# First norm's sums of ten tiles moved to ScalarE, the column tiling of chunk 1's projections dropped, another issue order

## The chip, the cores and the metric

One core of a Trainium2 chip. The metric is the device time of one execution in microseconds (us); a kernel is given by the median of its executions. PE is the matmul engine, DVE VectorE, ACT ScalarE, POOL GpSimd, SP the engine that issues transfers. All executions compared here were of the fast state (mean granted clock of PE, as a share of full speed, 0.98 to 1.00).

## The reference, cut to what matters

```python
mod = (_silu(c) @ w_mod).reshape(c.shape[0], 6, 1, -1)      # sa, ca, ga, sb, cb, gb
h = _layernorm(x, axis=-1) * (1 + ca) + sa                  # first norm, x is 2048 x 512
x = x + ga * _A_ref(h, A_wqkv, A_wo)                        # 32 heads, window of 8 keys, step 2
h = _layernorm(x, axis=-1) * (1 + cb) + sb                  # second norm
x = x + gb * _B_ref(h, B_w1, B_b1, B_w2, B_b2)              # a third norm, then an MLP over the rows
```

x is held as 16 tiles of 128 rows. Attention goes through five chunks of 2, 4, 4, 4 and 2 tiles. Its products (q by k, weights by v) are elementwise on DVE, which PE then sums up.

## The kernel before: the parts that matter

The kernel records every operation with a name and issues the operations in the order of one long string. A suffix picks an engine (`:a` ACT, `:d` DVE, `:p` POOL) or, for matmuls, `:q`: four column tiles side by side. Each engine takes its operations strictly in this order. In names, `ln1s4` is the statistics of tile 4 for the first norm, `n1_4` its normalisation, `qk1_0` a q-k product of chunk 1, `pv4_3` a product with v of chunk 4, `ev` an eviction from PSUM, `wsc` the scaling of a weight block, `x_1_4` a load of two tiles of x from tile 4.

```python
ORDER = """
ld_x_1_2 ident ld_c act_table ld_x_1_4 ld_x0 consts warm2 ld_x_2_8 ld_x1 cps ld_x_2_6 silu_exp ld_wmod1 ln1s3
...  (cut)
"""
    NE=('PAPADADAAADAAAPA', 'AAPPAPAAAAAAPAAA', 'APPAAADDDDDDDADD'),  # engine of each tile's normalisation, three norms
    VPOOL=(2, 3),                                                       # two blocks of the v weights scaled on POOL
...  (cut)
    def ln_stats(l, st, src, reads, name):
        st6, mv = ln_t["st6", l], ln_t["mv", l]

        def fd():
            nc.vector.bn_stats(st6[:, st, :], src)
            nc.vector.bn_aggr(mv[:, st, :], st6[:, st, :])
        return add("dve", 0.86, fd, reads=reads, writes=[("mv", l, st)], name=name)
...  (cut: ln_norm)
        alts = {"A": ("act", 0.8, lambda: nc.scalar.activation(dst, src, ACT.Identity, scale=r_, bias=n_)),
                "D": ("dve", 0.42, lambda: nc.vector.tensor_scalar(dst, src, args[0], args[1], op0=args[2], op1=args[3])),
                "P": ("pool", 0.8, lambda: nc.gpsimd.tensor_scalar(dst, src, args[0], args[1], op0=args[2], op1=args[3]))}
        G.add_any([alts[e]], reads=reads, writes=writes, name=name, locks=True)
```

Of the kernel before, what the change touches and what calls it, by code (L numbers as in the profile page):

```python
# [7 lines left out]
ACT = mybir.ActivationFunctionType  # L8
# [33 lines left out]
class _Graph:  # L42
# [7 lines left out]
    def add(self, eng, dur, fn, **kw):  # L50
        return self.add_any([(eng, dur, fn)], **kw)
# [131 lines left out]
ld_x_1_2 ident ld_c act_table ld_x_1_4 ld_x0 consts warm2 ld_x_2_8 ld_x1 cps ld_x_2_6 silu_exp ld_wmod1 ln1s3  # L183
ld_wqkv1 ln1s5 ld_wqkv0 ld_x_3_10 ln1s4 ln1s2 ln1s0 rstd1_1 ln1s1 ld_wmod0 ln1s9 rstd1_0 nb1_0 nb1_1 silu_dve
n1_1 n1_0 ld_x_4_14 ln1s6 n1_5 n1_2 fill:2:114 tr0_0 ln1s8 modcols1 n1_3 halo0 ld_wqkv2 n1_4 hT0_3:a hT0_1:d
hT0_0:a ld_x_3_12 fill:4:11 tr1_2 a1col hT0_2:d wsc1_0:a wsc1_1:d tr1_0 ld_wo3 wsc1_3:d wsc1_2:d hT1_3:a ln1s7
qkv0_12 hT1_1:a ld_wmod5 wsc0_0:a wsc0_1:d qkv0_10 wsc0_3:d ld_b2 rstd1_2 wsc0_2:d ln1s10 ld_wmod4 hT1_0:a
qkv0_00 ev0_10:a ln1s11 ev0_12:a modcols0 ld_wo0 nb1_2 qkv0_02 sab hT1_2:d ld_wmod3 n1_6 qvb0 ln1s15 qkv1_02
qvb_cp0 ln1s14 wsc2_2 ev0_02:a qvb1 ln1s13 wsc2_3 qkv1_10 wsc2_1:a wsc2_0:a qvb_cp1 qk0_3 qkv1_00 ev0_00:a
qkv0_22 qk0_2 ev1_02:a qkv1_01 ev1_10:a qk0_0 qkv0_20 ev1_01:a qk0_1 ev1_00:a red0_0 xt6 qkv1_12:q n1_9 qk1_0  # L190
ev0_20:a red0_1 red0_2 ld_wo1 red0_3 mask ev1_12:a ld_wmod2 qkv1_13:q n1_7 qkv1_03 max0 n1_8 xt7 qk1_2 qkv1_11
ev1_03:a xt9 sub0 qkv1_23 ev1_11:a exp0 qkv1_21 qk1_1 ev1_13:a xt8 ev0_22:a esum0 qkv1_22:q ld_b1 rcp0 halo_v1:p
rstd1_4 vd0_1 smB0 qkv1_20 qk1_3 a2_0_1 modcol2 a2_0_0 ev1_20:a red1_0 ev1_23:a a2_0_2 red1_1 ev1_22:a red1_2
a2_0_3 ln1s12 red1_3 ev1_21:a ld_wo2 qkv2_00 mcols0 nb1_4 max1 rstd1_3 n1_14 vd0_0 n1_15 qkv2_10 vd0_2 nb1_3
ev2_00:a n1_10 sub1 pv0_1 ev2_10:a xt10 qkv2_01 n1_12 qk2_0 mrowt0 qkv2_02 exp1 vd1_3 qkv2_11 vd0_3 ev2_01:a
n1_11 vd1_2 qkv2_22 pv0_2 ev2_11:a xt12 qkv2_12 mrows0:a ev2_02:a qk2_1 pvacc0_2 xt11 ev2_12:a red2_0 n1_13
esum1:q halo_v2:p xt13 qkv2_13:q rcp1 qk2_2 ev2_22:a qkv2_03:q vd1_1 ev2_13:a qkv2_23:q ev2_03:a smB1 qkv2_20:q
qk2_3 a2_1_3 red2_1 ev2_20:a a2_1_2 qkv3_01:q halo_k3:a ev2_23:a a2_1_0 red2_2 a2_1_1 qkv3_13 pv0_0 ld_w1_0_896
red2_3 st_row0 pv0_3 ev3_13:a qkv2_21:q vd1_0 max2 pvacc0_0 ev2_21:a qkv3_10:q pv1_3 pvacc0_1 sub2:q oev0_0:a
qkv3_23:q ev3_10:a exp2 qkv3_00:q ld_row0 pv1_2 xt14 ev3_01:a qkv3_02:q ev3_00:a qkv3_20:q vd2_0 ev3_23:a vd2_1  # L200
esum2:q pv1_0 ld_w1_0_0 qkv3_21 rcp2 pvacc0_3 qkv3_03:q woq_s oev0_2:a ev3_02:a pvacc1_3 ev3_03:a smB2 qkv3_11:q
pv1_1 a2_2_2 wo1:q ev3_11:a a2_2_1 ev3_21:a wo0 xt15 x1_1 halo_v3:a qk3_1 pvacc1_1 oev1_3:a a2_2_0 pvacc1_0 x1_0
a2_2_3 qkv3_12 oev1_1:a ld_w1_0_512 oev1_0:a qk3_0 pvacc1_2 vd2_2 modcol3 oev1_2:a vd2_3 ev3_12:a ln2q0 wo4
qk3_3 wo5 x1_4 ln2q1 qkv4_12 mcols1 ev3_20:a qk3_2 red3_0 ln2q4 red3_1 qkv3_22:q ln2m0 wo3 ev3_22:a pv2_1 x1_5
mrowt1 wo2:q mrows1:a x1_3 st_row1 red3_2 pv2_0 x1_2 pvacc2_1 rstd2_0 red3_3 ln2q2 qkv4_02:q oev2_1:a ld_row1
nb2_0 max3 n2_0 vd3_3 ev4_02:a vd3_0 pv2_3 sub3 vd3_2 qkv4_10 exp3 pvacc2_0 n2_1 esum3 pv2_2 ln2q3 qkv4_20
ev4_12:a qkv4_22:q rcp3 ev4_20:a ln2m2 pvacc2_2 aff0 warm3 oev2_0:a oev2_2:a qkv4_00:q smB3 rstd2_2 ln2q5 nb2_2
pvacc2_3 ln3s0 a2_3_1 n2_2 warm1 ev4_22:a a2_3_0 ln3s1 n2_3 biascols oev2_3:a a2_3_2 ln2m4 ev4_10:a aff2 wo7:q
a2_3_3 rstd2_4 ld_w2_1 rstd3_0 wo6:q nb2_4 nb3_0 ln3s2 n2_4 n2_5 h3_0 vd3_1 ln3s3 wo8:q h3_1 x1_6 aff4 warm0
rstd3_2 x1_7 wo9:q nb3_2 ln3s4 h3_2 h3_3 x1_8 ln3s5 halo_v4:p mlp1_0_2_0:q vd4_1 ev4_00:a pv3_0 mlp1_0_5_0:q  # L210
x1_9 mlp1_0_1_0:q rstd3_4 ln2q9 mlp1_0_0_0:q nb3_4 pv3_3 biascols_cp:a vd4_2 h3_5 pvacc3_0 h3_4 mlp1_0_6_0:q
ln2q8 mlp1_0_0_4:q pv3_2 mlp1_0_1_4:q vd4_3 park0_0:a mlp1_0_5_4:q mlp1_0_2_4:q park0_1:a mlp1_0_4_0:q ln2q7
park0_2:a pv3_1 mlp1_0_3_0:q vd4_0 ln2q6 mlp1_0_3_4:q oev3_0:a pvacc3_2 park0_3:a ld_w1_0_1152 pvacc3_3 oev3_2:a
ln2m6 mlp1_0_4_4:q qk4_0 oev3_3:a pvacc3_1 rstd2_6 mlp1_0_7_0:q oev3_1:a nb2_6 qk4_2 red4_0 n2_9 mlp1_0_6_4:q
wo13:q n2_7 qk4_1 ld_w1_0_1408 n2_6 wo12:q qk4_3 n2_8 park0_4:a red4_1 red4_2 aff6 red4_3 ld_w2_3 park0_5:a
wo11:q x1_12 mlp1_0_9_0:q ln2q12 park0_6:a wo10:q max4 x1_11 ld_w2_0 ln3s8 x1_13 sub4:q mlp1_0_10_0 ln3s7 exp4
x1_10 ln3s6 esum4 mlp1_0_11_0 ln3s9 rcp4 mlp1_0_12_0 smB4 rstd3_6 ln2m12 a2_4_3 ln2q10 h3_7 mlp1_0_8_0 h3_6
a2_4_1 rstd2_12 h3_8 mlp1_0_8_4 ln2q13 a2_4_2 nb2_12 h3_9 n2_12 ln2q11 a2_4_0 ln2m13 mlp1_0_9_4 ln2m10 rstd2_13
aff12 mlp1_0_7_4 rstd2_10 nb2_10 ln2m11 mlp1_0_7_8 ln3s12 rstd2_11 mlp1_0_8_8 n2_10 mlp1_0_9_8 pv4_0
ld_w1_0_1664 mlp1_0_11_4 park0_7:a rstd3_12 nb2_13 pv4_2 mlp1_0_10_4 park0_8:a n2_13 mlp1_0_10_8 nb2_11 pv4_1  # L220
mlp1_0_11_8 park0_9:a ld_w1_1_0 mlp1_0_12_4 park0_10:a pv4_3 mlp1_0_12_8 park0_11:a pvacc4_2 pvacc4_0 park0_12:a
aff10 pvacc4_1 pvacc4_3 n2_11 mlp1_0_13_0 aff13 ld_w2_5 oev4_0:a mlp1_0_13_4 aff11 oev4_2:a mlp1_0_13_8 inj1_0
wo15 ln3s10 wo14 ln3s13 rstd3_10 ln3s11 park0_13:a mlp1_1_0_6 x1_15 ld_w1_1_640 rstd3_13 ld_w1_1_896 rstd3_11
ln2s15 inj1_4 inj1_2 inj1_3 mlp1_1_3_6 nb3_13 h3_10 rstd2_15 nb2_15 mlp1_1_2_6 x1_14 n2_15 ln2s14 h3_13
mlp1_1_3_10 inj1_1 mlp1_1_0_10 mlp1_1_1_6 aff15 rstd2_14 nb2_14 mlp1_1_2_10 ln3s15 n2_14 mlp1_1_4_6 park1_0:a
h3_12 mlp1_1_1_10 aff14 inj1_5 rstd3_15 inj1_6 mlp1_1_4_10 mlp1_1_5_6 ln3s14 ld_w1_1_1408 mlp1_1_6_6 h3_11
rstd3_14 h3_15 park1_1:a h3_14 mlp1_1_6_10 mlp1_1_5_10 park1_2:a mlp1_1_10_10 ld_w1_2_0 park1_3:a mlp1_1_9_10
park1_4:a padd1_10 park1_5:a mlp1_1_7_10 park1_6:d ld_w2_7 mlp1_1_12_10 mlp1_1_8_10 padd1_12 padd1_9 mlp1_2_1_11
padd1_7 ld_w1_2_640 mlp1_2_1_14 gelu9 mlp1_2_2_11 gelu7 mlp1_2_4_11 ld_w2_4 gelu10 mlp1_2_4_14 mlp1_2_0_11
gelu12 padd2_4 mlp1_2_2_14 padd2_1 mlp1_2_0_14 padd2_2 mlp1_2_3_11 ld_w2_9 padd2_0 mlp1_2_3_14 gelu1 mlp1_2_6_11  # L230
padd1_8 gelu0 mlp1_2_5_11 padd2_6 gelu4 gelu2 mlp1_2_5_14 padd2_3 mlp1_1_13_10 padd2_5 gelu6 ld_w2_2 gelu8
mlp1_1_11_10 padd1_13 gelu5 gelu3 mlp2_0_0 padd1_11 gelu11 ld_w2_11 mlp2_0_0b gelu13 mlp2_0_0c mlp2_4_0 fin0_0
st_out0_0 mlp2_2_0 mlp2_8_0 fin2_0 fin4_0 st_out2_0 mlp2_1_0 st_out4_0 ld_w2_13 fin8_0 mlp2_7_0 fin1_0 st_out1_0
mlp2_5_0 st_out8_0 mlp2_11_0 mlp2_3_0 mlp2_6_0 fin3_0 fin5_0 st_out3_0 mlp2_9_0 st_out5_0 fin6_0 fin7_0
st_out6_0 ld_w2_15 mlp2_10_0 fin9_0 st_out9_0 st_out7_0 mlp2_14_0 fin10_0 st_out10_0 fin11_0 mlp2_12_0
st_out11_0 fin14_0 mlp2_13_0 st_out14_0 fin12_0 mlp2_15_0 fin13_0 mlp2_15_1 st_out13_0 fin15_0 st_out12_0
mlp2_15_2 fin15_1 st_out15_0 fin15_2 st_out15_1 st_out15_2
# [4 lines left out]
def kernel(  # L242
# [22 lines left out]
    NE=('PAPADADAAADAAAPA', 'AAPPAPAAAAAAPAAA', 'APPAAADDDDDDDADD'),  # L265
    X1D=(14, 15),
    LN2D=(14, 15),
# [100 lines left out]
    def ln_stats(l, st, src, reads, name):  # L368
        st6, mv = ln_t["st6", l], ln_t["mv", l]

        def fd():
            nc.vector.bn_stats(st6[:, st, :], src)
            nc.vector.bn_aggr(mv[:, st, :], st6[:, st, :])
        return add("dve", 0.86, fd, reads=reads, writes=[("mv", l, st)], name=name)
# [230 lines left out]
    def build_chunk(ch):  # L605
# [26 lines left out]
        if ch in XDMA:  # L632
            first = None
            for sl, st in enumerate(tiles):
                dma_t = lambda sl=sl, st=st: nc.sync.dma_start_transpose(out=hT[:, :, sl * P:(sl + 1) * P],
                                                                         in_=h3[:, st, :])
                add("sp", 1.25, dma_t, reads=[("n1", st)] + ([("hT_raw", bh)] if sl else []),
                    writes=[("hTr", ch, sl)] + ([] if sl else [("hT_raw", bh)]), bytes_=0.5, lat=1.2, desc=8,
                    name=f"xt{st}")
# [378 lines left out]
```

## Time and profile before

| | before |
|---|---|
| time, median of the first 3 executions | 207.41 us (207.18 to 207.63) |
| profiled span | 205.1 us |

The busy times and PE's standstill before stand in the prediction below. A busy time is the sum of an engine's instructions. Two groups by shape that the prediction doesn't show, of the kernel before (after the bars: busy us, mean ns, then the idle time ahead of them and what ended it):

```profile
L133 POOL TENSOR_SCALAR h<-xx,rs,nb 128x512 bf16<-128x512 bf16 x7 | 5.4, 780 | 73.2 <-DVE nb L133 73.2
L133 DVE TENSOR_TENSOR big<-q_sb,k_f 128x2048 bf16<-128x2048 bf16 x8 | 9.3, 1220 | 0.0
```

POOL does nine normalisations here, the seven of this group at 0.78 us each, and the q-k products of two tiles take DVE 1.22 us.

### The profile page before, as it was taken

The numbers are of one execution on the slowest core, as the hardware profiler recorded it, in microseconds if no ns is written. First come the engines' busy times: TensorE is split into PE (matmuls) and PEld (weight loads), VectorE is DVE, ScalarE is ACT, GpSimd is POOL, SyncE is SP. The second block draws the span as 40 slices with busy tenths as digits, with TensorE's granted clock in tenths as the row PEclk, the third lists the DMA queues.
The fourth block names the chain that finished last, engine by engine and source line by source line (L and its number), as shares of the span: only waits on it lengthen the run. The fifth ranks groups of instructions, "written<-read, shape, count | busy, mean of one in ns | idle before, by whom it ended". The sixth has DMA issues, their size and how long they took to land.

```text
span 205.1 us, 5082 instructions
## 1 busy us (share of the span) xinstructions
PE 196.7 (96%) x2089; PEld 106.7 (52%) x2089; DVE 162.6 (79%) x258; ACT 118.0 (58%) x271; POOL 15.4 (7%) x36
## 2 busy tenths in 40 slices
PE   7999999997999997999999999999999999999994
PEld 6988654453553644644555444444444444444453
DVE  2989999999999999999999899964563262066845
ACT  2396897983768788989999796673682000000000
POOL 4112007120000000230000100000000000000000
PEclk9999999999999999999999999999999999999999
DMA  5999684796859839073389149559992045006202
GB/s 170 303 375 298 156 174 113 219 261 183 247 180 283 243 141 357 27 190 147 121 220 219 27 97 336 187 125 291 274 300 67 29 135 146 0 26 165 81 26 78
DMA packets 55114, 35.98 MB, mean 175 GB/s; under 512 B 24628, under 2 KB 52404, under 8 KB 55092
## 3 DMA queue, kind: packets, MB, share of 16 engines
q1 hardware_dynamic: 55084, 35.67, 63.1%
q8 instruction: 16, 0.26, 0.5%
q14 instruction: 6, 0.05, 0.1%
q10 hardware_dynamic: 8, 0.00, 0.0%
HBM read 22.55 MB, written 2.10 MB: 120 GB/s over the span
## 4 chain that ended last, share of the span: by engine, by line
PE 52%; DVE 31%; issue 6%; ACT 5%; DMA 3%; SPq 2%; DVEq 0%
PE psS L133 50%; DVE big L133 17%; DVE h L133 5%; DVE st L133 4%; DVE mv L133 2%; PE psL L133 2%; ACT h L133 2%; SPq L133 2%; DMA xx<-in_A_x_dram 1%; DMA a2sb<-lsb 1%; ACT xx L133 1%; DVE lsb L133 1%; DVE m L133 1%; ACT q_sb L133 1%; DVE nb L133 0%
## 5 line engine op out<-in xcount | busy, mean ns | idle before, releaser
L133 PE MATMUL psS<-h,wst 128*32 128x512 bf16 (+1 forms) x374 | 51.1, 379 | 0.4 <-POOL h L133 0.2
L133 PE MATMUL psS<-hT,w_qkv 128*32 128x512 bf16 (+3 forms) x516 | 46.9, 346 | 1.5 <-ACT v_sb L133 1.1
L133 PEld LDWEIGHTS <-wst 128*128 128x128 bf16 (+1 forms) x476 | 29.6, 98 | 30.2 <-issue 2.2
L133 PEld LDWEIGHTS <-w_qkv 128*32 128x32 bf16 (+1 forms) x558 | 29.8, 109 | 22.3 <-issue 3.8
L133 DVE TENSOR_TENSOR big<-a2sb,vD 128x4096 bf16<-128x4096 bf16 (+1 forms) x20 | 36.5, 1861 | 0.2
L133 DVE TENSOR_TENSOR big<-q_sb,k_f 128x4096 bf16<-128x4096 bf16 (+1 forms) x20 | 36.4, 1861 | 0.0
L133 DVE SCALAR_TENSOR_TENSOR h<-psS,bcol,rows_bc 128x512 f32<-128x512 f32 (+2 forms) x18 | 12.4, 691 | 23.2 <-PE psS L133 22.9
L133 PE MATMUL psS<-gT,big 128*128 128x512 bf16 x112 | 24.8, 379 | 0.0
L133 PEld LDWEIGHTS <-ident 128*128 128x128 bf16 (+1 forms) x301 | 15.5, 104 | 6.7 <-issue 2.1
L133 PEld LDWEIGHTS <-big 128*128 128x128 bf16 x144 | 12.0, 98 | 13.2
L133 ACT ACTIVATE h<-xx,nb,rs 128x512 bf16<-128x512 bf16 x22 | 17.2, 808 | 1.7 <-DVE nb L133 1.7
L133 PE MATMUL psS<-woq,o_sb 128*32 128x512 bf16 (+1 forms) x184 | 16.5, 380 | 0.4 <-ACT xx L133 0.4
L133 DVE TENSOR_TENSOR psS<-psS,gT 128x512 f32<-128x512 f32 x14 | 9.0, 694 | 8.0 <-PE psS L133 8.0
L133 DVE BATCH_NORM_STATS2 st<-xx 128x6 f32<-128x512 bf16 x18 | 12.2, 677 | 3.8 <-DMA xx<-in_A_x_dram 3.7
L133 ACT ACTIVATE v_sb<-psS,qvb 128x512 bf16<-128x512 f32 (+1 forms) x20 | 11.2, 598 | 4.3 <-PE psS L133 4.2
L133 ACT ACTIVATE lv<-mv,epscol 128x1 f32<-128x1 f32 (+2 forms) x25 | 7.3, 292 | 11.0 <-DVE mv L133 10.8
L133 PE MATMUL psS<-ident 128*128 128x128 bf16 x161 | 12.0, 242 | 1.4 <-POOL epscol L133 1.4
L133 ACT ACTIVATE q_sb<-psS,qvb 128x512 bf16<-128x512 f32 (+1 forms) x20 | 11.1, 599 | 2.8 <-DVE qvb L133 1.9
L133 DVE TENSOR_TENSOR h<-h,xx 128x512 bf16<-128x512 f32 (+2 forms) x18 | 11.4, 632 | 1.6 <-DMA out_dram<-h 1.0
L133 ACT ACTIVATE gT<-psS,bcol 128x512 bf16<-128x512 f32 x14 | 8.7, 684 | 7.0 <-DVE psS L133 7.0
L133 DVE TENSOR_TENSOR h<-h,rows_bc 128x512 bf16<-128x512 bf16 (+2 forms) x20 | 11.5, 581 | 0.3
L133 PEld LDWEIGHTS <-group 128*32 128x32 bf16 x288 | 7.0, 96 | 8.8 <-issue 2.7
(89 smaller groups left out, 213.9 us busy)
## 6 DMA issues: line engine op xcount, KB each, us to landing
vD<-v_sb SPq DMA_DIRECT2D x12, 524.5 KB, 4.6
big<-in_B_w_dram SPq DMA_DIRECT2D x4, 896.0 KB, 8.1
vD<-v_sb SPq DMA_DIRECT2D x8, 268.5 KB, 2.6
wst<-in_B_w_dram SPq DMA_DIRECT2D x3, 640.0 KB, 4.4
out_dram<-h SPq DMA_DIRECT2D x15, 128.0 KB, 1.8
xx<-in_A_x_dram SPq DMA_DIRECT2D x7, 256.0 KB, 6.9
wst<-in_B_w_dram SPq DMA_DIRECT2D x2, 800.0 KB, 4.8
gT<-in_w_mod_dram SPq DMA_DIRECT2D x3, 512.0 KB, 8.3
```

Source lines behind the costliest of these rows:

```text
L133: r = fn(*a, **k)
```

## The change

Its intent: ACT stands idle for half of the first 20 us while DVE is full; so let ACT make the sums of ten tiles of x by two passes (the mean, the mean of squares), and let DVE only combine them. The order and the engine letters are new throughout; the three column-tiled projections of the first two chunks, all of chunk 1, run at full width.

```diff
-ld_x_1_2 ident ld_c act_table ld_x_1_4 ld_x0 consts warm2 ld_x_2_8 ld_x1 cps ld_x_2_6 silu_exp ld_wmod1 ln1s3
+ld_c ld_x_1_4 ident act_table ld_x_1_2 ld_x0 consts warm2 ld_x_2_6 ld_x_2_8 cps ld_x1 ld_wmod1 ln1s5 halo0
 ...  (cut: the rest of the order)
-    NE=('PAPADADAAADAAAPA', 'AAPPAPAAAAAAPAAA', 'APPAAADDDDDDDADD'),
+    NE=('DDPDPDAAAPADPAAA', 'PAPPAPAAAAAAAPPA', 'PAPAAADDAPDADPDP'),
+    LN1A=(4, 5, 6, 7, 8, 9, 10, 11, 12, 13),
 ...  (cut)
+        if l == 0 and st in LN1A:
+            def fa():
+                nc.scalar.activation(junk[:], src, ACT.Identity, scale=1.0 / D, accum_out=mv[:, st, 0:1])
+                nc.scalar.activation(junk[:], src, ACT.Square, scale=D ** -0.5, accum_out=st6[:, st, 0:1])
+            add("act", 1.36, fa, reads=reads + ["act_table"], writes=[("sq", l, st)], name=name)
+            add("dve", 0.15, lambda: nc.vector.scalar_tensor_tensor(
+                mv[:, st, 1:2], mv[:, st, 0:1], mv[:, st, 0:1], st6[:, st, 0:1], op0=ALU.mult, op1=ALU.subtract,
+                reverse1=True), reads=[("sq", l, st)], writes=[("mv", l, st)], name="ln1v" + name[4:])
+            return
 ...  (cut: options that stay unused, estimates of durations)
```

## The prediction

> **What bounds the kernel now.** I read four views of the profile before, in this order: the busy table, a table of engine times in stretches of 5 us, the chain of waits, and the groups by shape.
>
> ```profile
> PE 196.7 (96%) x2089; PEld 106.7 (52%) x2089; DVE 162.6 (79%) x258; ACT 118.0 (58%) x271; POOL 15.4 (7%) x36
> ```
> PE looks full and DVE four fifths full, but these are means over stages. The stretches (columns: stretch, its length, then PE, PEld, DVE, ACT, POOL busy, granted clock, DMA share, GB/s) tell the stages apart:
> ```profile
> 5.00:10.00 5.00, 5.00 (x85) 5.00 (x83) 4.72 (x18) 1.55 (x5) 0.47 (x1) 1.00 0.95 298
> ...
> 15.00:20.00 5.00, 5.00 (x77) 4.37 (x75) 4.86 (x16) 3.05 (x8) 1.16 (x2) 1.00 1.11 306
> ...
> 35.00:40.00 5.00, 5.00 (x30) 2.36 (x23) 4.93 (x9) 4.86 (x10) 0.76 (x1) 1.00 0.64 180
> ...
> 160.00:165.00 5.00, 5.00 (x25) 2.28 (x24) 2.13 (x3) 0.00 (x0) 0.00 (x0) 1.00 0.01 2
> ```
> DVE is full from 3.7 us to about 136 us and half idle after it. ACT is idle half the time in the first 20 us (1.55 and 3.05 of 5) but full at 35 to 40. That hole is what the change wants to fill. The chain of waits (start, length, what) agrees at both ends:
> ```profile
> 3.71 0.70 DVE st L133
> 4.41 0.02 issue
> 4.43 0.18 DVE mv L133
> 4.62 0.59 DVE st L133
> ...
> 123.50 75.54 PE psS L133 x355
> ```
> The first norm's sums stand on the chain at once when x lands (0.59 + 0.20 us a tile, seven tiles to 9.4 us). From 123.5 us the chain is 75.5 us of matmuls back to back, 355 of them at 0.213 us: nothing but less matmul work after that point, or an earlier start of it, shortens it. The start is when DVE has done the last product of chunk 4.
>
> How much can PE gain at all? Adding the starts of neighbouring matmuls in the timeline, PE stands still for only some 6.3 us in all; the two largest are these:
> ```profile
> 48.38 1.06 PE L133 MATMUL psS<-hT,w_qkv 128*32 128x512 bf16 x16 [1.06 <-ACT v_sb L133]
> ...
> 78.55 0.59 PE L133 MATMUL psL<-m,nident 128*128 128x512 bf16 x2 [1.49 <-DVE m L133]
> ```
> and it loses about 0.09 us at each of some 30 changes between full-width and column-tiled matmuls (2.7 us), and about 10 us to filler matmuls on the identity at the start. So no more than 6 to 8 us can be won by any reordering, and DVE and PE are close to co-bound before 123 us.
>
> **What the Trainium skill says.** "ScalarE: Activation LUTs", section What ACT_TABLE_LOAD costs, gives an ACTIVATE with immediate scale and bias as 186 ns + 0.833 ns per column, and 93 ns of overlap between neighbours: 613 ns at 512 columns. The trace agrees: the second norm's Square pass takes 622 ns and starts 0.62 us before the next instruction with its accumulator read counted.
> ```profile
> L133 ACT ACTIVATE junk<-xx 128x512 bf16<-128x512 bf16 x14 | 8.7, 622 | 0.1
> L133 ACT ACTIVATION_READ_ACCUMULATOR junk<-xx 128x1 f32 x14 | 2.7, 192 | 0.0
> L133 DVE BATCH_NORM_STATS2 st<-xx 128x6 f32<-128x512 bf16 x18 | 12.2, 677 | 3.8 <-DMA xx<-in_A_x_dram 3.7
> L133 DVE CAST gT<-psS 128x512 bf16<-128x512 f32 x1 | 0.7, 680 | 0.0
> ```
> "TensorEngine Tiling (Array Packing)", Key Properties, says that a change of tiling mode drains the array; the 0.09 us per change is what the trace shows of it. "Trainium Kernel Development and Optimization", Performance Expectations, calls matmul busy time a bad metric; here 96% does overstate, though by little. "DMA: Bandwidth & Descriptors", section Queues, rings and completion order, says that each of the 16 engines takes descriptors in ring order. The trace fits: in the order of issue the x tiles landed at 4.38 (512 KB in all by then), 6.57 (896 KB), 7.04 (1024 KB) and 8.60 us (1280 KB).
>
> **The change part by part.**
>
> *DVE.* Up to the last attention product (chunk 4) I count its instructions in the two orders and price them by the spacing in the trace. Ten pairs of BN statistics go: 10 x 0.80 = -8.0. Ten one-column variance instructions come (like the one-column ones at about 150 ns, spaced 0.13): +1.3. Four evictions of q and k from PSUM move from ACT to DVE: 4 x 0.68 = +2.7. Two more transposed chunk-1 copies (0.33), two more first-norm applications (0.38), one more weight scaling (0.26): +1.7. Two fewer third-norm applications: -0.6. Sum -2.9 us out of 117.9. So most of what ACT takes over is handed back.
>
> *ACT.* +10 x 1.23 = 12.3 us; minus 4 normalisations (2.8), 2 copies (0.95), 2 evictions (1.2), 1 scaling (0.6): +6.7 us before the second exp, which started at 38.4 us. Before that ACT had idle: about 4.2 + 1.0 + 1.9 and smaller ones. After it there is nearly none left: ACT becomes a second full engine from 10 to 40 us.
>
> *PE.* The same products. Three more filler matmuls at 0.07: +0.2. Changes of mode fall from 32 to 26: -0.6. Behind the last attention reduction stand five 512-column matmuls fewer (4 of one MLP block, 1 injection): -5 x 0.2155 = -1.1 us after the point where DVE lets go. Without column tiling in chunks 0 and 1 the columns streamed are equal, since four tiles run side by side.
>
> *Front end, worked by hand.* Before: the first transposes begin at 10.5 us, when the filler ends; the first product of q and k on DVE at 20.3, that of chunk 1 at 24.9. After: tile 1, which chunk 0 needs, is the sixth x load instead of the fifth. By bytes it lands at about 8.3 instead of 7.0. Its statistics end at 9.1, both rstd on ACT at 10.1, four normalisations on DVE and POOL at 11.4: the transposes begin 0.5 to 1 us later. Then ACT runs two more tiles of sums ahead of the chunk-0 copies, and one (tile 7, 1.23 us) ahead of a q weight scaling; the second projection waits for that, up to 1 us. Against this, DVE is free sooner and evicts q and k of chunk 0 itself, so the first q-k product comes at 18.5 to 20 us. The gain is then used up by evictions and waits for ACT. I get chunk 1's first product between 23.4 and 25.6, against 24.9.
>
> *Middle.* From chunk 1 on both kernels keep DVE full: one pair less (-0.8), four variance instructions (+0.4) and one eviction (+0.7) more: +0.3. Two normalisations fewer near the end: -0.6.
>
> *Sum.* If all DVE savings became time: -2.9 at the handover, -1.1 behind it: -4.0. Pessimistic: front end +0.7, middle +0.3, and the PE queue full since chunk 4's reductions so that the -1.1 and -0.6 don't show: +1.0. I take -1.0 us: 206.4.
>
> **The rivals.**
>
> 1. *ACT becomes the bound in the front end.* For it: the 4.86 of 5 above at 35 to 40 us, +6.7 us of work, and sums placed before copies that PE waits for. Against it: idle time of about that size, and evictions handed to DVE. It would make the time 207 to 209.
> 2. *PE is the bound and a DVE saving is hidden.* For it: only 6.3 us of standstill in 200; from 97 us on hardly 0.6. Against: the two largest standstills wait on DVE and ACT, and removing them would give 1 to 2.5 us. It would make the time 206 to 207.
> 3. *The DVE saving arrives in full*, if x tile 1 lands in time and the front end keeps ahead: 203.4 to 205.
> 4. *A late transfer.* The last w2 block and the attention's small transfers are issued in another order; a late one would stall PE in the tail, where it is never idle now. It would cost 1 to 2 us; loads are issued many us ahead, so I give it little.
>
> **Range and chances.** Median 206.4. The sums span 203.4 (rival 3) to 209 (rivals 1 and 4); 204.0 to 208.8 should hold it 8 times in 10. Faster by over 2% means under 203.3, at the edge of rival 3: 0.09. Slower by over 2% means over 211.6, beyond all sums: 0.03. Within 2%: 0.88.
>
> **What would show each step.** Right: BN statistics of x fall from 18 to 8, twenty sum passes of about 0.6 us appear on ACT; DVE's busy time falls by about 3 us and ACT's rises by about 6 to 7 us; ACT nearly full from 10 to 40 us; DVE idle for 1 to 3 us between 7 and 16 us where it was full; the first transposes start at 11 to 11.5 us; chunk 1's first product at 23.4 to 25.6; the long last run of matmuls starts near 122 to 123. Wrong: if the transposes begin at 10.5 as before and chunk 1's first product comes before 23 us, the front end was misjudged and the time falls to 204; if PE idles over 2 us before 25 us or over 1 us after 123 us, rival 1 or 4 holds and the time rises to 208 or above.

## The result, and the profile after

After: **209.35 us** median (209.18 to 209.62, 5 executions), before 207.31 us (206.72 to 207.63, 5). The ratio is 1.0101, 95% interval 1.0082 to 1.0121. The kernel before was run again beside every batch below (medians 207.14 to 207.68 us). Ratios here are the mean time of one kernel's fast runs over that of the other's in the same rounds, so not quite the ratio of the medians. The kernel became 2.0 us slower, outside the predicted range (204.0 to 208.8).

The busy table and groups of the kernel after, to be held against those of before:

```profile
PE 196.6 (95%) x1987; PEld 106.8 (51%) x1987; DVE 164.0 (79%) x257; ACT 124.1 (60%) x298; POOL 24.0 (12%) x41
...
L133 DVE BATCH_NORM_STATS2 st<-xx 128x6 f32<-128x512 bf16 x8 | 5.5, 681 | 4.8 <-DMA xx<-in_A_x_dram 4.7
L133 DVE TENSOR_TENSOR big<-q_sb,k_f 128x2048 bf16<-128x2048 bf16 x8 | 9.9, 1280 | 0.1
...
L133 ACT ACTIVATE junk<-xx 128x512 bf16<-128x512 bf16 x34 | 21.3, 626 | 1.5 <-DMA xx<-in_A_x_dram 1.0
...
L133 POOL TENSOR_SCALAR h<-xx,rs,nb 128x512 bf16<-128x512 bf16 x10 | 10.7, 1069 | 62.0 <-DVE nb L133 54.8 <-DVE qvb L133 6.3 <-DVE mv L133 0.9
```

The statistics fell from 18 to 8 and twenty passes came to ACT, as intended. But DVE is busier than before (164.0 against 162.6), and two groups have become slower per piece: POOL's normalisations (1069 ns against 780) and DVE's two-tile products (1280 against 1220, eight pieces of one size). Something stretches both.

The same view by stretches as the prediction shows it, of the kernel after:

```profile
5.00:10.00 5.00, 5.00 (x78) 5.00 (x76) 3.90 (x16) 4.62 (x18) 0.40 (x1) 1.00 1.02 344
...
15.00:20.00 5.00, 5.00 (x64) 4.03 (x62) 4.83 (x12) 4.81 (x13) 2.26 (x3) 1.00 1.11 295
...
80.00:90.00 10.00, 8.34 (x123) 5.26 (x124) 9.65 (x17) 7.90 (x25) 3.32 (x3) 1.00 0.55 189
```

ACT's hole in the front is filled (1.55 to 4.62, 3.05 to 4.81). From 80 to 90 us PE is now busy for 8.34 us. Before, it was for all 10:

```profile
80.00:90.00 10.00, 10.00 (x192) 6.21 (x192) 9.62 (x21) 9.17 (x25) 2.84 (x4) 1.00 0.35 117
```

The end of the chain of waits after:

```profile
136.18 0.89 DVE h L133
137.09 0.71 DVE st L133
138.57 0.71 ACT h L133
139.32 64.99 PE psS L133 x328
```

The unbroken last run of matmuls begins at 139.3 us, after PE stood 0.60 us for the last normalised rows; before it began at 123.5. Where the lag arises is read from the ends of operations that both kernels have (us):

| end of the operation | before | after | lag |
|---|---|---|---|
| first product of chunk 1 | 27.15 | 28.06 | 0.91 |
| maximum of chunk 1 | 36.76 | 38.13 | 1.37 |
| last q-k product of chunk 4 | 107.26 | 109.12 | 1.86 |
| last product with v | 123.45 | 125.72 | 2.27 |
| last third-norm rows on DVE | 136.83 | 139.29 | 2.46 |

To find what is stretched I took each DVE instruction's duration less the lower quartile of all instructions of its shape in the two traces, and kept what exceeds 0.1 us. Before: one instruction, 0.31 us in all. After: eight, **3.18 us** in all, every one of them while POOL ran: two normalisations at 10 us (0.30, 0.46), a q-k product at 18.5 (0.49), two small sums at 80.5 and 86.4 (0.31 each), three operations of the second and third norm at 85.0, 116.5 and 136.2 (0.47, 0.38, 0.46). A ninth, a weight scaling at 20.2 us (0.79 us, where six others of its shape take 0.35), is the only one of its name in the two traces and so is missing from the sum. Four of the eight (10.1, 18.5, 85.0 and 86.4 us) met operations that are POOL's in the kernel before too: there the new order, and not a new letter, brought the two together. Besides, DVE waits once for a result of POOL (0.72 us at 118 us). That gave the first theory.

In 26 of the 71 executions of the kernel after and its variants the mean granted clock was 0.98 to 0.99, in none of the 85 of the kernel before and its variants below. Four profiles (k6, k10, k13, k15) show where: PE's clock is at half for 3.4 us, beginning at 80.7 to 81.9 us, behind a stretch in which PE mostly stood still. What this costs was not tested. It doesn't explain the loss: the kernel after took 209.18 to 209.40 us in its four executions at 1.00 and 209.62 us in the one at 0.99, and its profile is at 1.00.

### The profile page after: what moved, and what is told of

It reads as the page before. It is cut to its first block, busy times and chain, and to the rows that moved or that the text cites. A ratio compares the mean times of both kernels' runs of the same rounds, so it can differ in the third digit from the quotient of the medians.

```text
span 207.7 us, 4902 instructions
## 1 busy us (share of the span) xinstructions
PE 196.6 (95%) x1987; PEld 106.8 (51%) x1987; DVE 164.0 (79%) x257; ACT 124.1 (60%) x298; POOL 24.0 (12%) x41
## 4 chain that ended last, share of the span: by engine, by line
PE 50%; DVE 33%; ACT 9%; issue 4%; DMA 1%; SPq 1%; POOL 1%; DVEq 0%; POOLq 0%; ACTq 0%
PE psS L133 48%; DVE big L133 17%; DVE h L133 5%; DVE st L133 5%; DVE mv L133 2%; ACT junk L133 2%; PE psL L133 2%; ACT h L133 2%; ACT xx L133 1%; DMA a2sb<-lsb 1%; DVE m L133 1%; ACT lv L133 1%; ACT rs L133 1%; SPq L133 1%; DVE xx L133 1%
## 5 line engine op out<-in xcount | busy, mean ns | idle before, releaser
L133 PE MATMUL psS<-h,wst 128*128 128x512 bf16 (+1 forms) x254 | 50.9, 379 | 1.2 <-POOL h L133 0.8
L133 PEld LDWEIGHTS <-wst 128*128 128x128 bf16 (+1 forms) x356 | 28.7, 98 | 31.7 <-issue 2.7
L133 ACT ACTIVATE junk<-xx 128x512 bf16<-128x512 bf16 x34 | 21.3, 626 | 1.5 <-DMA xx<-in_A_x_dram 1.0
L133 PEld LDWEIGHTS <-ident 128*128 128x128 bf16 (+1 forms) x280 | 16.1, 106 | 6.3 <-issue 1.7
L133 POOL TENSOR_SCALAR h<-xx,rs,nb 128x512 bf16<-128x512 bf16 x10 | 10.7, 1069 | 62.0 <-DVE nb L133 54.8
L133 ACT ACTIVATE h<-xx,nb,rs 128x512 bf16<-128x512 bf16 x17 | 13.3, 808 | 1.1 <-DVE nb L133 1.1
L133 PE MATMUL psS<-ident 128*128 128x128 bf16 x164 | 12.6, 246 | 1.4 <-POOL epscol L133 1.4
L133 DVE TENSOR_TENSOR h<-h,rows_bc 128x512 bf16<-128x512 bf16 (+2 forms) x20 | 12.4, 625 | 1.1 <-POOL h L133 0.7
L133 ACT ACTIVATE v_sb<-psS,qvb 128x512 bf16<-128x512 f32 (+1 forms) x19 | 10.6, 597 | 3.4 <-PE psS L133 3.4
L133 PE MATMUL psS<-big,group 128*32 128x512 bf16 (+1 forms) x160 | 9.2, 338 | 3.0 <-DVE big L133 3.0
```

Source lines behind the costliest of these rows:

```text
L133: r = fn(*a, **k)
```

## The experiments

**Theory A**: DVE pays for POOL. **Rivals**: B, DVE is simply the bound and the sums on ACT are the wrong trade; C, the matmuls without column tiling cost time; D, the front is held by ACT, by the arrival of x, or by PE's filler matmuls. "Stretch" below is the sum defined above.

### A1. Collisions taken out of the middle and the end (k1_mid)

```diff
-    NE=('DDPDPDAAAPADPAAA', 'PAPPAPAAAAAAAPPA', 'PAPAAADDAPDADPDP'),
+    NE=('DDPDPDAAAPADPAAA', 'AAPPAPAAAAAAAPPA', 'PAPAAADDAADADPDD'),
 order: nb2_2 moved behind aff0, so that POOL's n2_2 and n2_3 run beside statistics; ln2m4 behind ln3s1; nb3_15 out
```

> The changed kernel with five collisions of POOL and DVE taken away from 75 us on: tile 0's second-norm application and tile 9's third-norm application go from POOL to ACT, tile 15's from POOL to DVE, and the second-norm scaling of tiles 0 and 1 stands ahead of the instruction that lets POOL start on tiles 2 and 3, which then run beside BN statistics. Contention theory: five DVE instructions lose 1.9 us of stretch, so the time falls by 1.3 to 2 us to about 207.5. Rival (ACT is late since the sums are on it): ACT gets two applications (1.4 us) more, so the time stays at 209.4 or rises.

208.42 us (207.86 to 209.06), ratio to before 1.0061 (1.0025 to 1.0097), stretch 0.75 us. The stretch fell by 2.4 us, the time by 0.9 us only, less than the 1.3 to 2 us expected (A4 shows two waits that were left). In the profile after, POOL (first line) and DVE (the others) at 84 to 87 us; columns are start, length, engine, operation:

```profile
84.50 2.33 POOL L133 TENSOR_SCALAR h<-xx,rs,nb 128x512 bf16<-128x512 bf16 x2 [3.51 <-DVE nb L133]
...
84.32 1.86 DVE L133 TENSOR_TENSOR h<-h,rows_bc 128x1024 bf16<-128x1024 bf16 x2
86.36 0.47 DVE L133 TENSOR_TENSOR mv<-mv,sums 128x2 f32<-128x2 f32 x1
```

The same operations in this run:

```profile
84.87 1.52 POOL L133 TENSOR_SCALAR h<-xx,rs,nb 128x512 bf16<-128x512 bf16 x2 [33.01 <-DVE nb L133]
...
83.28 1.41 DVE L133 TENSOR_TENSOR h<-h,rows_bc 128x1024 bf16<-128x1024 bf16 x2
84.73 0.69 DVE L133 BATCH_NORM_STATS2 st<-h 128x6 f32<-128x512 bf16 x1
86.58 0.16 DVE L133 TENSOR_TENSOR mv<-mv,sums 128x2 f32<-128x2 f32 x1
```

POOL's pair now takes 1.52 instead of 2.33 us, DVE's pair 1.41 instead of 1.86 and the small sum 0.16 instead of 0.47, while the statistics that now run beside POOL keep their 0.69. The Trainium skill, page "SBUF — State Buffer", section SBUF: two separate sides, says why: GpSimd and VectorE share a port pair as an exclusive lock; a VectorE instruction competes for it if it has two SBUF inputs or runs in a two-port mode. This trace agrees in kind; the price here is 0.3 to 0.5 us for a DVE instruction hit. Three of the eight stretched ones (10.1, 10.7 and 116.5 us) are normalisations that read one tile only; the trace doesn't show whether they ran in such a mode.

The page also says that whichever starts first keeps the pair. The front shows it by accident. After, the first of two POOL operations begins 0.05 us ahead of DVE's product:

```profile
18.49 2.33 POOL L133 TENSOR_SCALAR w_qkv<-h,a1col 128x512 bf16<-128x512 bf16 x2
...
18.54 1.71 DVE L133 TENSOR_TENSOR big<-q_sb,k_f 128x2048 bf16<-128x2048 bf16 x1
```

In this run its weights landed later, and DVE came first:

```profile
18.77 2.15 POOL L133 TENSOR_SCALAR w_qkv<-h,a1col 128x512 bf16<-128x512 bf16 x2 [0.36 <-DMA h<-in_A_wqkv_dram]
...
18.43 1.23 DVE L133 TENSOR_TENSOR big<-q_sb,k_f 128x2048 bf16<-128x2048 bf16 x1
```

The product takes 1.23 us instead of 1.71. So a part of the cost depends on when a transfer lands.

### A2. The same, dosed into the kernel before (k4_pool_dose)

```diff
+        if ch < 3:
+            for i_ in range(2):
+                add("pool", 0.8, lambda: nc.gpsimd.tensor_scalar(junkp[:], lsb_r[b][:, 0:512], a1col[:, 0:1], 0.0,
+                                                                 op0=ALU.mult, op1=ALU.add), ..., name=f"dum{ch}_{i_}")
```

> The kernel before with six POOL instructions more (128x512, SBUF to SBUF), two after each of the attention-weight scalings of chunks 0, 1 and 2, which nobody waits for. Contention theory: each pair stretches the DVE products beside it by 0.4 to 0.8 us in all, so DVE's busy time rises by 1.2 to 2.4 us and the time by 1 to 2 us to 208.4 to 209.4. Rival (POOL is free): under 0.2 us.

207.97 us, ratio 1.0033 (0.9998 to 1.0068), profiled span 206.4 against 205.1. Stretch rose from 0.31 to 1.46 us. DVE's busy time rose from 162.6 to 163.6 us, just under what was expected, the time (0.6 us) well under, and the interval doesn't tell it from nothing. Four of the six operations were held up themselves (1.54 to 4.72 us each, the other two took 0.69). In the profiles the way from the end of chunk 1's first product to the end of the last product with v grew from 96.30 to 97.16 us. It supports the theory weakly.

### A3. The front's POOL operations put on DVE (k7_front_dve)

```diff
-    NE=('DDPDPDAAAPADPAAA', ...      VPOOL=(2, 3),
+    NE=('DDDDDDAAADADPAAA', ...      VPOOL=(),          # and wsc2_2:d wsc2_3:d, nb1_1 out
```

> The kernel after with the five POOL operations of the front (three normalisations, two weight scalings) put on DVE, and one small DVE instruction less. Contention theory: DVE loses 0.30, 0.46 and 0.49 us (and up to 0.44 us at a scaling) to them, and doing them itself costs 3 x 0.33 + 2 x 0.26 - 0.13 = 1.4 us, so the offload bought nearly nothing: the first product of chunk 1 ends within 0.4 us of the kernel after's 28.06 us, the time within 0.5 us of 209.35. Rival, POOL's help is free: DVE falls 1.2 to 1.5 us behind, chunk 1's first product ends at 29.3 to 29.6 and the time is 210.5 to 210.9. In both no DVE instruction before 28 us is stretched.

209.33 us, ratio 1.0110 (1.0089 to 1.0131): the time of the kernel after. Chunk 1's first product ends at 28.07 us (28.06 after). Five operations more on DVE cost it nothing, since it had paid nearly as much in stretch (1.25 us in the sum, and the scaling at 20.2 us). So in the front POOL's help was worth nothing, and taking it away gains nothing. The skill's page "Perfetto Trace Analysis", section Optimizing Scalar/DVE Operations, warns that moving work between GPSIMD and DVE might not help; here it is shown with numbers.

### A4. Two waits ahead of the last product with v (k13_mid2), and no collision anywhere (k14_mid2_front)

The first run still had two waits there, one for POOL, which the kernel after has too, and one of my own making, as the normalisation that I had moved to ACT stood ahead of an rstd:

```profile
116.61 0.16 DVE L133 SCALAR_TENSOR_TENSOR nb<-sums,rs 128x1 f32<-128x1 f32 x1 [1.09 <-ACT rs L133]
...
117.74 0.89 DVE L133 TENSOR_TENSOR h<-h,rows_bc 128x512 bf16<-128x512 bf16 x2 [0.71 <-POOL h L133]
```

```diff
 k13, from k1:  NE second norm, tile 13  P -> D;  third norm, tile 9  A -> D
 k14, from k13: the edit of A3 as well
```

> The first run's kernel (208.42 us) with two normalisations just ahead of the last attention product on DVE (0.33 us each) in place of ACT and POOL; they made DVE wait 1.09 and 0.71 us in its profile. If the time is set by DVE up to that product, which ended 1.16 us later than in the kernel before, the product ends 1.1 us earlier, level with before, and the time is 207.2 to 207.9. If PE's queue is full there, or the front holds the rest, it stays at 208.1 to 208.7.

> The same with the five POOL operations of the front on DVE as well, so no DVE instruction of it is stretched at all. The run that did this alone to the kernel after changed nothing (209.33 us), so I expect the time of the kernel beside it within 0.4 us. If instead the collision at chunk 0's product, which falls in some executions and not in others, is a part of the rest, it is faster by 0.4 us or more.

| kernel | time, us | ratio to before (95%) | stretch, us |
|---|---|---|---|
| after | 209.35 | 1.0101 (1.0082 to 1.0121) | 3.18 |
| k1 | 208.42 | 1.0061 (1.0025 to 1.0097) | 0.75 |
| k13 | 207.92 | 1.0019 (0.9987 to 1.0052) | 1.24 |
| k14 | 207.62 | 1.0007 (0.9978 to 1.0037) | 0.00 |

With POOL out of DVE's way the changed kernel is level with the kernel before. The step from k13 to k14 is inside the intervals. DVE's busy time in k14 is 162.7 us, that of before to 0.1 us; up to the last product with v it is 116.0 us against 116.8. So with DVE doing this work itself, the change spares it under 1 us there, and nothing in all. (The product of A1 collided again in k13's profile, so k13 has more stretch than k1.)

The expectation for k13 failed in one point: the last product with v ended at 125.01 us, not 1.1 us earlier than in k1 (124.61), as in that profile the statistics of tile 1 of x began 0.8 us later and chunk 1's first product ended at 28.71 instead of 27.43 us. Measured from that end on, the way to the end of the last product with v is 96.30 us before, 97.66 after, 97.19 in k1, 96.30 in k13 and 96.31 in k14. So all that the kernel after lost on this way, 1.36 us, came back when POOL's operations and the two waits were out of the way. The lag of the front (0.91 us after, 1.27 in k14) did not.

### B. Are the sums on ACT the wrong trade?

```diff
 k3:  LN1A=()                                        # all ten back on DVE, the rest as after
 k12: LN1A=(4, 5, 6, 10, 11, 12, 13)                 # three back on DVE
 k11: ev0_12:a ev0_10:a ev0_02:a ev1_21:a            # four evictions back on ACT
```

> The changed kernel with the ten tiles' sums back on DVE and nothing else undone: ten BN pairs (8 us) for ten one-column instructions (about 1.7). DVE is the bound: the time rises by 4 to 6 us to 213 to 215. Rival (ACT's 14 us of sums hold up the front end): the time falls to 207 to 209, near the kernel before.

> The kernel after with the sums of tiles 7, 8 and 9 back on DVE, at the same places of the order. DVE gets 3 x 0.67 = 2.0 us more before 16 us, where it stood idle for 1.6 us, ACT is spared 4.4 us there. If DVE alone sets the front, half of that or more shows: chunk 1's first product ends at 29 us or later, time 210 to 211.4. If ACT is as much of a bound, the gain on ACT pays for it: the product ends within 0.5 us of 28.06 us and the time is 208.8 to 209.9.

> The kernel after with one part undone: the four evictions of q and k that had moved to DVE are back on ACT, at the same places of the order. DVE is spared 4 x 0.61 = 2.4 us, ACT gets about 2.4 us. If DVE alone sets the front and the early middle, the kernel gains 1 to 2.4 us: 207.0 to 208.4. If ACT, which has no idle time from 9.2 to 29 us in the kernel after, is as much of a bound there, the three evictions of chunk 0 wait behind sums and the first product waits for them: chunk 0's first product starts later than 18.54 us, chunk 1's first product ends at 28 us or later and the time is 209.2 to 211. I expect the second.

k3 213.07 us (ratio 1.0273, 1.0245 to 1.0302), k12 210.43 (1.0137, 1.0093 to 1.0180), k11 210.87 (1.0145, 1.0100 to 1.0191). In the changed order, DVE can't take all sums back (k3 +3.7 us on the medians). Three of them (k12, +1.1 us), or the evictions back on ACT (k11, +1.5, though DVE is spared 2.4 us of work), gain nothing either; that they cost is less sure, since both intervals overlap with that of the kernel after (1.0082 to 1.0121). k11's waits on DVE name the engine (us in total, times, longest):

```profile
DVE big L133 <- ACT q_sb L133: 1.9, 3, 1.2
```

k12's time is in the range of a DVE bound, though its end of chunk 1's first product, 28.84 us, lies between my two hypotheses; k11's time is in the range of an ACT bound. This fits two engines that are both full in the front. One caution: tile 1 of x landed late in k11's profile (its statistics began at 8.62 us, 7.34 after), so the profile of k11 shows two causes at once.

### C. The column tiling (k5_before_noq, k6_after_q, k5b_noq_vd)

```diff
 k5 (from before): -qkv1_12:q -qkv1_13:q -qkv1_22:q   +qkv1_12 +qkv1_13 +qkv1_22
 k6 (from after):  the reverse
 k5b:              k5, and vd1_0 (a transfer of v) issued ahead of ld_w1_0_896 and st_row0
```

> The kernel before with its three column-tiled projections of chunks 0 and 1 at full width, the other named part of the change alone. I expect under 0.5 us either way: four more changes of tiling mode at 0.09 us. Rival (the column tiling in the first chunks was worth the loss): slower by 1.5 to 2 us.

> The kernel after with the column tiling of the three chunk-1 products restored, the other direction of the run that took it away from the kernel before. If column tiling is worth something by itself (the 1.5 us by which the kernel before grew without it), this one gains 1 to 1.5 us: 207.8 to 208.4. If it is worth nothing and the 1.5 us there came from two transfers that happened to land about 1 us later, this one stays within 0.4 us of the kernel after: 209.0 to 209.8. I expect the second.

> The kernel before without the column tiling of the three chunk-1 products, as run already (208.87 us), and with the transfer of v that came late there issued ahead of the weight load and the row store that stood before it. If the late landings explain the 1.5 us, the wait of 0.80 us at chunk 1's first product with v is gone and the time is 207.4 to 208.1. If the missing tiling itself costs time, it stays at 208.5 to 209.2.

k5 208.87 us (1.0072, 1.0041 to 1.0103): a miss, 1.5 us slower. k6 209.49 (1.0109): no difference from after, so in this order the tiling is worth nothing measurable. What k5 lost stands in its waits, two small transfers that landed about 1 us later than before:

```profile
DVE big L133 <- DMA a2sb<-lsb: 1.1, 1, 1.1
DVE big L133 <- DMA vD<-v_sb: 0.8, 1, 0.8
```

In k5b the second was gone and another came in its place, as the row store that I had put behind it now went out later, and the load that reads it as well:

```profile
DVE woq L133 <- DMA rows_bc<-scratch: 2.1, 1, 2.1
DVE big L133 <- DMA a2sb<-lsb: 0.9, 1, 0.9
```

Time 209.97 us (1.0144): the expected gain failed. In these two runs the transfers around 50 to 65 us had no slack, and one or another was exposed. Why the dropped tiling shifts them stays open; the kernel after has no wait of DVE for a transfer from 17 to 127 us, so this is no part of its loss.

### D. What holds the front? (k9, k9b, k10, k15 to k18)

```diff
 k9  (before): LN1A=(4, 5, 13), ln1s13 behind ev0_12      k9b (before): LN1A=(4, 5), ln1s8 and ln1s7 moved up
 k10 (k1):     sums of 7, 8, 9, 12 back on DVE; four evictions, one copy, three POOL normalisations to ACT
 k15 (k14):    ld_x1 fourth, ln1s6 behind rstd1_1, tr0_0 ahead of modcols1
 k16 (k15):    fill:2:114 -> fill:2:100
 k17 (k16), k18 (k15): ln1s9 ln1s8 ln1s7 behind ACT's copies hT0_2 hT0_3 and wsc1_3; ln1s12 later
```

> The kernel before with one part of the change alone, and that only where ACT stands idle: the sums of tiles 4, 5 (ACT idle from 3 to 7 us) and 13 (idle from 16.8 to 18.7 us) on ACT, three small instructions on DVE. DVE is spared 3 x 0.80 - 3 x 0.13 = 2.0 us before chunk 0's first product. If DVE's work in the front sets the time there, the first product of chunk 1 (27.15 us in the kernel before) ends 1.2 to 2 us earlier and the time falls by 0.7 to 1.8 us, to 205.6 to 206.7, unless the products then meet POOL's two weight scalings at 19 to 20 us (0.5 us lost). If the arrival of x and the PE set the front, the product ends within 0.4 us and the time stays 207.0 to 207.6.

208.96 us (1.0081): failed by my placing. Tile 13 landed at 18.9 us and ACT stood waiting for it, ahead of an eviction (the wait in k9's profile):

```profile
ACT junk L133 <- DMA xx<-in_A_x_dram: 2.4, 1, 2.4
```

Then the small variance instruction, which I had put behind a maximum, delayed the next rstd as well.

> The kernel before with the sums of tiles 4 and 5 alone on ACT, in its idle time from 3 to 7 us, two small instructions on DVE, and the statistics of tiles 8 and 7 moved up into the time that this frees. DVE is spared 1.3 us. The earlier try with three tiles failed by its third: ACT stood 2.4 us waiting for tile 13 of x (landed 18.9 us) ahead of an eviction. If the landing of x sets the front (tile 13 lands at 19.4 us in the kernel before and its statistics end at 20.3 us, just ahead of chunk 0's first product), nothing moves: chunk 1's first product ends within 0.2 us of 27.15 us and the time is 207.0 to 207.5. If DVE's work sets it, the product ends 0.6 to 1.3 us earlier and the time is 206.0 to 206.8.

208.43 us (1.0034, 0.9994 to 1.0074): no gain. The tile-8 statistics that I moved up began only at 7.45 us, when their tile had landed, and tile 1's behind them ended 0.57 us later than before; chunk 1's first product ended 0.46 us later. Time freed on DVE ahead of the arrival of x can't be used.

> An attempt at a version that beats both kernels: the kernel after without the POOL collisions of the middle and the end (as in the first run, 208.42 us), and ScalarE's time spent where it spares DVE most. A sum on ACT costs it 1.46 us and spares DVE 0.67 us; an eviction or a transposed copy costs ACT 0.5 to 0.6 us and spares DVE 0.33 to 0.68 us. So the sums of tiles 7, 8, 9 and 12 go back to DVE (+2.7 us there, -5.8 us on ACT) and four evictions, one copy and the three POOL normalisations of the front go to ACT (about -2.9 us on DVE, -0.8 us of stretch, +5 us on ACT). Theory: DVE ends chunk 1's first product at 26.6 to 27.1 us (27.43 in the first run, 27.15 in the kernel before) and the time is 207.0 to 207.8, level with the kernel before or slightly below. Rival: ACT's queue, full in both, delays an eviction and the product stays at 27.4 or later, time 208.2 to 209.

209.75 us (1.0116): the rival's case or worse. Stretch by the sum above was nil, but DVE waited 2.8 us for ACT's rstd instead.

> The collision-free version (207.62 us) with tile 1 of x as the fourth load instead of the sixth, its statistics ahead of the sums of tile 6, and the first transposes ahead of the modulation's 16 small matmuls, as in the kernel before. The transposes then start when the 114 filler matmuls end, at 10.0 to 11.1 us. If tile 1's arrival held the front, chunk 1's first product ends 0.5 to 1 us earlier (28.42 us there) and the time is 206.6 to 207.2, below both kernels. If the fillers or ACT hold it, the time is 207.3 to 207.9.

> The same with 100 filler matmuls instead of 114, 1.0 us less at 0.07 us each, on PE ahead of the first transposes. If the fillers set the start of the transposes, it gains up to another 1 us: 205.8 to 206.6. If the normalised tiles come no earlier than the fillers end, or the matmuls after them run slower for it, it is level with the other of this pair within 0.3 us or above it.

k15 208.11 us (1.0024), above both ranges that I gave; k16 207.98 (1.0019), level with it, as its second case has it. Neither is below before. In k16 the transposes of chunk 0 had ended by 10.4 us, but ACT had sums in its queue first. In its profile, ACT copies the transposes at 13.0 us, DVE waits for that, PE for DVE's weights:

```profile
12.97 0.64 ACT L133 ACTIVATE hT<-psS 128x256 bf16<-128x256 bf16 x2
...
13.64 0.29 DVE L133 COPY hT<-psS 128x256 bf16<-128x256 bf16 x1 [1.62 <-ACT hT L133]
...
14.38 1.83 PE L133 MATMUL psS<-hT,w_qkv 128*128 128x256 bf16 x15 [1.80 <-DVE w_qkv L133]
```

> The version with tile 1 early and 100 fillers (207.98 us) with ACT's sums of tiles 9, 8 and 7 put behind its copies of the transposes and a weight scaling, and the sums of tile 12 behind the first evictions. If the sums ahead of the copies hold the front, the first projection starts near 12.5 instead of 14.4 us, chunk 1's first product ends 0.8 to 1.8 us earlier (28.53 us there) and the time is 206.2 to 207.2, below the kernel before. If the landing of the q weights (13.8 us) or ACT's total work holds it, the gain stays under 0.5 us: 207.5 to 208.1.

> The same with 114 fillers. The transposes then start when these end, 10.0 to 11.0 us. If the first projection still starts before 13.3 us, it is within 0.4 us of the other; if the fillers now stand on the path, it is 0.5 to 1 us slower.

k17 208.30 us (1.0064), above both ranges that I gave, and k18 208.56 (1.0070), within 0.4 us of it: ACT's copies began at 11.8 instead of 13.0 us in k17 and the first product of chunk 0 0.9 us earlier (18.57 against 19.45), but the sums, now behind it, delayed the next rstd (DVE waited 0.6 us), PE waited 1.4 us for an eviction, and chunk 1's first product ended at 28.87 instead of 28.53 us. The ten tiles' sums, some 14 to 15 us, have to be done by ACT somewhere ahead of 36 us, and every place I tried costs. No version beat the kernel before; the best, k14, equals it.

## Why the prediction was wrong, point by point

**The failed step** is the pricing of DVE: instructions counted "in the two orders" and priced "by the spacing in the trace", "Sum -2.9 us". The spacings were those of instructions beside which POOL mostly stood still. I counted the normalisations that left DVE and ACT as pure gain ("Two fewer third-norm applications: -0.6", "minus 4 normalisations (2.8)") without asking where they went and what would run beside them. Of the two third-norm ones, tile 8 went to ACT and tile 9 to POOL; in all ten went to POOL, and the new order laid four of these and four older POOL operations beside DVE operations that were stretched. DVE's work up to the last product with v was to fall by 2.9 us. It took 117.1 us against 116.8 before; without the stretch it would have been about 2.2 us less, so the count itself was 0.7 us too good.

At the last product with v DVE was to be 2.9 us early and was 2.27 us late. Of these 5.2 us the traces show 2.4 as stretch up to there (2.72 against 0.31), 0.7 as the wait for POOL's result, 0.6 as a later start (the first statistics begin at 4.33 instead of 3.71 us, as their tiles are now the second load) and 1.2 as waits between 7 and 16 us (1.6 against 0.4); 0.3 are left. So most of the term that I left out is POOL, and none of my four rivals was. Removing the collisions and the wait for POOL brought the ratio from 1.0101 to 1.0019 and 1.0007, so this cause is shown for 0.8 of the 1.0%; the rest is within the intervals. The 1.25 us of stretch in the front are not a loss of their own, as A3 shows: they are the price of POOL's help there. What holds the front's lag of 0.9 us, the later start and the waits, is read from the traces; k15 to k18 changed the loads, the fillers and ACT's order, and did not win it back.

**ACT**: "+6.7 us" was about right in sum (busy 118.0 to 124.1) and wrong in the term. (Of the "four evictions of q and k" one is of v.) A tile's sums cost 1.50 us in a row and 1.39 alone, not 1.23, as here in the kernel after:

```profile
3.64 0.63 ACT L133 ACTIVATE junk<-xx 128x512 bf16<-128x512 bf16 x1 [0.95 <-DMA xx<-in_A_x_dram]
4.17 0.18 ACT L133 ACTIVATION_READ_ACCUMULATOR junk<-xx 128x1 f32 x1
4.39 0.63 ACT L133 ACTIVATE junk<-xx 128x512 bf16<-128x512 bf16 x1
4.93 0.19 ACT L133 ACTIVATION_READ_ACCUMULATOR junk<-xx 128x1 f32 x1
5.14 0.63 ACT L133 ACTIVATE junk<-xx 128x512 bf16<-128x512 bf16 x1
```

Passes one behind the other start every 0.75 us, and the next one begins only after the accumulator is read (0.19 us). The 0.62 us that I took came from passes followed by other work. Why a second pass waits longer is not shown: an eviction into x with an accumulator of its own starts 0.61 us after a pass that began at 81.9 us, so it is not the accumulator alone; both passes write the same tile. It comes to some 2 us over ten tiles, most of it in ACT's full stretch.

**Front end**: transposes "0.5 to 1 us later": right (11.33 against 10.51 us), but by luck. Tile 1 landed at about 7.3 us, not 8.3; PE reached the transposes later because its fillers ran to 11.1 instead of 10.7 us, as PE's clock rose from half to full at 6.7 instead of 5.8 us in these two profiles, and because the modulation's matmuls now stood ahead. In k7, with the same loads, they began at 10.34 us, and chunk 1's first product ended no earlier. "ACT nearly full from 10 to 40 us" and "DVE idle for 1 to 3 us between 7 and 16 us" (1.6) were right, and so was the first q-k product "at 18.5 to 20 us" (18.54). Chunk 1's first product "between 23.4 and 25.6" began at 25.74, just outside on the late side.

**PE**: mode changes fell from 32 to 26 in the traces, as forecast, and matmuls behind the last attention reduction are 384 instead of 389 (76.8 against 77.9 us at 0.2157 us for 512 columns): "-1.1" was right. But these five only moved ahead of that reduction, and 0.60 us came back at 138.5 us as a wait for the last normalised rows.

**Middle** "+0.3, -0.6": wrong. The lag grew from 1.1 us (at 40 us) to 1.9 (at 97 us), with 1.1 us of stretch from 80 to 87 us on the way; PE's standstill from 60 to 90 us grew from 2.0 to 5.0 us.

**Rivals**: 1, ACT as a second bound of the front: k11 and k16 show DVE waiting for it (1.9 and 1.6 us), but POOL, not ACT, made the loss that A4 won back. 2, a full PE hides the saving, had no saving to hide. 3 didn't happen. 4, a late transfer, did not happen in the kernel after, but did in k5 and k5b. Of the signs of error, "PE idles over 2 us before 25 us or over 1 us after 123 us" did not show (at most 1.1, and 0.6 us), yet the time rose above 208: I had looked for the loss at both ends, and most of it was in between.

## What to carry to other kernels

Work on POOL is free only beside DVE instructions that don't need its port, and only if DVE doesn't wait for the result; ask of each POOL operation which DVE instruction will run beside it, and compare durations of one shape, not only busy sums. A new order can bring the two together as well as a new engine. Count where removed work went before counting it as saved. In a kernel tuned until two engines are full together, moving work between them needs a price in both, with the spacing measured in the pattern in which it will run.

## What the Trainium skill lacked or had wrong

- "SBUF — State Buffer", Who interferes with whom: it has the lock and which operations take it, and the traces agree. It lacks the price in a tuned kernel: 0.3 to 0.5 us for each of the eight stretched DVE instructions of the kernel after, and more for POOL (a normalisation of 2.67 us instead of 0.77 at 78.3 us, an operation of 4.72 instead of 0.69 in k4).
- "ScalarE: Activation LUTs", What ACT_TABLE_LOAD costs: it has no figure for the accumulator read, which took 0.19 us here. A pass and its read overlap as the page says (the read starts 0.54 us into a pass of 0.63), but of two passes one behind the other the second starts after 0.75 us.
- "TensorEngine Tiling (Array Packing)", Key Properties: the drain at a change of mode has no figure there; here about 0.09 us each; restoring the tiling of three products made no difference in k6 (209.49 against 209.35 us).
- "TensorE: Matmul & The Clock Gate", Part 1: it has a change of the matmuls' pace some time into the kernel, varying by 500 ns either way from run to run. Here the spacing of the same 114 fillers fell from 107 to 56 ns anywhere from 4.4 us (k4) to 7.5 us (k9b), so their end moved between 10.0 and 11.5 us.
- No page that I read says how far the landing of a load at the start of a kernel varies from one execution to the next: with the load order of the kernel after, the statistics of tile 1 of x began at 7.34 us (after) to 8.62 us (k11).
